# A decode block on one core: first loads issued ahead of the critical section, the store waited for by ScalarE behind it

## The chip, the cores and the metric

The kernel runs on one core of one Trainium2 chip. The metric is the device time of one execution in microseconds. The kernel before takes 400.61 us in the median of three runs (400.36 to 400.88). One execution was profiled; all rows below come from it.

## What is computed

One token (batch 1, sequence 1, D = 1024) goes through a residual sum of two branches, both fed by the layernorm of `x`: attention over a key/value cache of 65,536 positions with 32 query heads on 4 key/value heads of 128, and an MLP mixer with its own layernorm.

```python
xn = _layernorm(x, axis=-1)
return x + _A_ref(xn, A_k_cache, A_v_cache, A_wq, A_wo) + _B_ref(xn, B_w1, B_w2, B_w3, B_w4)

# _A_ref: q = xn @ wq; scores = q k^T * Dh**-0.5; p = softmax(scores); o = p v; o @ wo
# _B_ref: h = gelu(layernorm(xn) @ w1), its four quarters shifted along the sequence, @ w2 = hs
#         (with one position each shift leaves only the zeros of the padding);
#         x1 = xn + hs;  x1 + gelu(layernorm(x1) @ w3) @ w4
```

Everything is bf16 in memory. The caches hold 134 MB and the weights some 35 MB, and each byte is used once.

## The kernel before, in words

The five engines are programmed by hand inside one critical section (`tile_critical`, line 226): semaphores are waited for and counted by the helper class `Flow`. Its method `one` records an instruction of VectorE (V), ScalarE (S) or GpSimd (G); `dma` (line 99, the issue is line 102) a transfer issued by an engine's queue, which adds 16 to a semaphore named by `lane` when it has landed; `_wait` (the wait is line 71) puts a wait ahead of an instruction when it reads or overwrites something that another engine or a transfer has still to finish. TensorE's program is written separately (`tensor_program`, from line 279) as loops that take tokens.

SBUF holds three slots of 32,768 bf16 per partition (64 KB a partition, 8 MB each): C, A, B. All large data passes through them, and SP issues all large loads, in this order: wq into A; w3 into C; the larger part of w4, and w2, into B; then, when wq has been used, w1 and the first rows of w4 into A; when w3 has been used, the first K tile into C; then V, K, K, V and so on by tiles of 32,768 keys (`load_tile`); last, wo in seven pieces into C. A load waits on SP until the products that read the slot's old content have ended (`load`).

The input `x` is loaded twice, both on ScalarE's queue: as one row of 1024 on one partition (`xr`, 2 KB in one piece), and in columns (`x_bf`, 128 partitions of 8 elements, 16 bytes each). From the row, ScalarE, GpSimd and VectorE make the mean and the variance of two nested layernorms (lines 408 to 418), TensorE spreads the four numbers to all partitions (line 281), ScalarE copies them out (line 422). GpSimd then normalises the columns (line 423) into `xn` and `cols`, and gives TensorE a token as soon as these and wq are there. TensorE multiplies by wq (line 286, `row_product` with A), then by w3 (again line 286, with C), and later the other weights (line 307); then come the eight K/V tiles (lines 330 and 345), wo (lines 307, 363, 367), a copy by ScalarE (line 599) and the store (`out`, ScalarE's queue).

Around the section stand parts that the framework makes: a start barrier of all engines behind four memsets (attributed to line 620), the section's entry (a NOP on SP, on which the other engines' branch into the section waits, lines 226 and 631), its exit (a drain of each engine but GpSimd, waits on SP, a NOP on GpSimd and one on SP, line 226), and the final barriers (line 631). The last thing that GpSimd does in the section is to wait until the store has landed.

## Time and profile before

| what | value |
|---|---|
| median of 3 runs | 400.61 us |
| the profiled execution | 400.84 us |
| its span, first to last instruction | 398.7 us |
| TensorE, VectorE, ScalarE, GpSimd busy | 251.5, 205.7, 48.9, 19.1 us |
| moved from HBM | 169.87 MB, 426 GB/s over the span |
| wq load: issued, landed | 0.95, 22.90 us |
| row of x: issued, landed | 0.90, 2.58 us |
| columns of x: issued, landed | 1.49, 25.00 us |
| store: issued, landed | 396.03, 397.70 us |
| granted TensorE clock, mean | 0.867 |

In the timeline, a row holds start, duration, engine, line, operation, what it writes and reads, count, and in brackets the idle time of the engine before it and what ended it; `SPq` and `ACTq` are the sequencers that issue transfers. In the windows, a row holds the window, its length, busy time of PE, PEld, DVE, ACT and POOL with their instruction counts, the granted clock, the DMA share and GB/s. In the DMA view, q1 is SP's queue and q10 ScalarE's, with packets, megabytes and the time that the packets took as a share of the 16 engines. A wait's row holds who waited for whom, the total in us, how often, and the longest.

### The profile page before, as it was taken

What the parts mean: (1) busy time and instruction counts of PE and PEld (TensorE: products, weight loads), DVE (VectorE), ACT (ScalarE), POOL (GpSimd) and SP (SyncE); (2) the same over time, 40 slices, a digit from 0 to 9 for tenths busy, and PEclk for the clock granted to TensorE, in tenths of its full rate; (3) what the DMA queues carried; (4) which work ended last, traced back from release to release, by engine and by line L of the source; (5) the groups of instructions that cost most, each with busy time, mean ns of one, the idle gap of its engine ahead of it and who ended that gap; (6) DMA issues with size and microseconds to landing.
All of it is one profiled execution on the core that took longest, in us unless ns stands there. A gap on an engine that the chain in (4) does not pass through costs nothing. (4 is left out here: it accounts for less than half of the span.)

```text
span 398.7 us, 4662 instructions
## 1 busy us (share of the span) xinstructions
PE 251.5 (63%) x1458; PEld 115.5 (29%) x1458; DVE 205.7 (52%) x135; ACT 48.9 (12%) x87; POOL 19.1 (5%) x58
## 2 busy tenths in 40 slices
PE   0039781997860985198429833981598169779685
PEld 0014330443340432044104411440244024423341
DVE  0000603039625954695079428940993398598510
ACT  5200117200020011002000200020003000300301
POOL 4030000000000003000000030000002000000000
PEclk9999995899985898599858985997698759989999
DMA  8999999999999999999999999999999999999995
GB/s 349 460 401 447 394 436 459 421 421 480 460 427 421 421 421 421 421 487 460 421 421 421 421 421 421 487 460 421 421 421 421 421 427 454 434 421 421 437 423 244
DMA packets 4618, 169.88 MB, mean 426 GB/s; under 512 B 645, under 2 KB 649, under 8 KB 906
## 3 DMA queue, kind: packets, MB, share of 16 engines
q1 hardware_dynamic: 4464, 169.87, 98.7%
q10 hardware_dynamic: 154, 0.01, 0.0%
HBM read 169.87 MB, written 0.00 MB: 426 GB/s over the span
## 5 line engine op out<-in xcount | busy, mean ns | idle before, releaser
L546 DVE STREAM_TRANSPOSE home<-home 128x4096 f32<-128x4096 f32 (+1 forms) x41 | 140.0, 3475 | 68.2 <-DMA home<-in_A_k_cache_dram 68.2
L330 PE MATMUL banks<-home,qst 128*128 x512 | 126.6, 409 | 76.8 <-PEq L277 76.4
L330 PEld LDWEIGHTS banks<-home,qst 128*128 128x128 bf16 x512 | 52.1, 102 | 150.8 <-issue 99.3
L554 ACT ACTIVATE scratch<-m 1x128 f32<-1x128 f32 x8 | 2.5, 308 | 244.7 <-DVE m L553 244.7
L345 PE MATMUL banks<-home,scratch 128*32 128x512 bf16 x512 | 31.4, 398 | 1.4 <-PEq L277 1.2
L307 PE MATMUL banks<-home,cols 128*33 x128 | 29.8, 392 | 2.5 <-PEq L277 2.5
L564 DVE STREAM_TRANSPOSE scratch<-scratch 128x1024 bf16<-128x1024 bf16 x16 | 19.9, 1245 | 17.1 <-ACT scratch L560 17.1
L319 PE MATMUL banks<-ident_f 128*128 128x128 f32 x118 | 26.0, 348 | 0.0
L286 PE MATMUL banks<-home,xn 128*33 x64 | 16.0, 418 | 12.4 <-PEq L277 12.4
L319 PEld LDWEIGHTS banks<-ident_f 128*128 128x128 f32 x118 | 19.3, 213 | 5.2 <-issue 1.2
L345 PEld LDWEIGHTS banks<-home,scratch 128*32 128x32 bf16 x512 | 15.0, 101 | 15.4 <-issue 6.0
L307 PEld LDWEIGHTS banks<-home,cols 128*33 x128 | 12.8, 100 | 18.9 <-issue 6.2
L560 ACT ACTIVATE scratch<-banks,sm 128x1024 bf16<-128x1024 f32 x16 | 17.8, 1113 | 0.5
L463 DVE CAST scratch<-banks 1x2048 bf16<-1x2048 f32 x1 | 2.3, 2279 | 29.2 <-PE banks L286 29.2
L474 POOL COPY qst<-qsel 32x32 bf16<-32x32 bf16 x16 | 3.3, 205 | 268.7 <-DVE sm L512 239.6
L550 DVE TENSOR_REDUCE sm<-banks 128x1 f32<-128x1536 f32 x8 | 13.9, 1738 | 1.2 <-PE banks L330 1.2
L286 PE MATMUL banks<-home,cols 128*33 x56 | 12.2, 379 | 3.0 <-PEq L277 3.0
L286 PEld LDWEIGHTS banks<-home,xn 128*33 128x33 bf16 x64 | 6.8, 106 | 21.3 <-issue 14.9
L551 DVE TENSOR_REDUCE sm<-banks 128x1 f32<-128x512 f32 x8 | 5.5, 692 | 12.6 <-PE banks L330 12.6
L526 DVE SCALAR_TENSOR_TENSOR scratch<-banks,sm,scratch 128x128 f32<-128x128 f32 x16 | 5.6, 350 | 12.0 <-POOL scratch L522 6.5
L487 DVE STREAM_TRANSPOSE scratch<-scratch 32x3584 bf16<-32x3584 bf16 x1 | 3.9, 3899 | 13.5 <-ACT scratch L480 13.5
L281 PE MATMUL banks<-sm,ident_f 1*128 1x4 f32 x2 | 0.6, 345 | 13.7 <-PEq L277 13.7
(91 smaller groups left out, 83.7 us busy)
## 6 DMA issues: line engine op xcount, KB each, us to landing
home<-in_A_k_cache_dram SPq DMA_DIRECT2D x2, 4096.0 KB, 40.8
home<-in_A_v_cache_dram SPq DMA_DIRECT2D x2, 4096.0 KB, 22.3
home<-in_B_w_dram SPq DMA_DIRECT2D x1, 7168.0 KB, 38.4
home<-in_B_w_dram SPq DMA_DIRECT2D x1, 6144.0 KB, 52.5
home<-in_B_w_dram SPq DMA_DIRECT2D x2, 2048.0 KB, 39.1
home<-in_A_wo_dram SPq DMA_DIRECT2D x2, 2048.0 KB, 33.5
home<-in_A_wo_dram SPq DMA_DIRECT2D x3, 1024.0 KB, 39.7
home<-in_B_w_dram SPq DMA_DIRECT2D x1, 1024.0 KB, 23.3
```

What stands on the lines that cost most here:

```text
L286: ins = te.matmul(banks[0:33, bank:][:, bass.ds(ch, 1), :], lhsT=lhsT[:, c:c + 1].to_broadcast([P, 33]), rhs=slot(s)[:, bass.ds(ch * 512 + ...
L307: ins = te.matmul(dst(h), lhsT=lv[:, u:][:, bass.ds(c, 1)].to_broadcast([P, 33]), rhs=wv[:, u * NOUT + h * NH:][:, bass.ds(c * NOUT, NH)], ...
L319: te.matmul(bank[:, 0:P], lhsT=ident_f[:], rhs=ident_f[:], start=True, stop=True, skip_group_check=True)
L330: ins = te.matmul(sc[:, bass.ds(hf, 1), :], lhsT=qst[:, bp, 24 - 8 * cg:24 - 8 * cg + P], rhs=kv[:, bass.ds(r * (2 * 4 * HF) + hf * 4 + cg ...
L345: ins = te.matmul(oacc[32 * u:32 * (u + 1), :], lhsT=work[:, 32 * y:32 * (y + 1)], rhs=vt[:, hf, :, t, :], start=(y < 4), stop=(y >= 60), ...
L487: v(["row0"], ["turned"], lambda e: e.transpose(out=rows32[:, 0:F], in_=rows32[:, 0:F]), tok="VT", peek=["rep4"])
L526: v(["oacc", "wm", "og"], ["og"], lambda e: e.scalar_tensor_tensor(out=og[:, 0:P], in0=oacc[:, P * cg:P * (cg + 1)], scalar=wm[:, 1, cg:cg ...
L546: v([], [("kt", ks, hf)], lambda e: e.transpose(out=part, in_=part), tok="VT", n=n, peek=[("slot", ks, piece_of("K", t, hf)), "qst"], guar ...
L550: v(SC[0:3] + ["sm0"], ["mx2"], lambda e: e.reduce_max(out=mx2[:, 0:1], in_=sc[:, 0:3, :].rearrange("p h n -> p (h n)"), axis=AX.X))
L551: v(SC[3:4], ["mx2b"], lambda e: e.reduce_max(out=mx2[:, 1:2], in_=sc[:, 3, :], axis=AX.X), tok="VT", guard=["pm"])
L560: s(SC + [("nball", r)], [("work", h), "row0", "row1", "turned", ("lall", r, h)], lambda e: e.activation(out=workv[:, 2 * h:2 * h + 2], in ...
L564: v([("work", h)], [("work", h)], lambda e: e.transpose(out=workv[:, 2 * h:2 * h + 2], in_=workv[:, 2 * h:2 * h + 2]))
```

## The change

Three loads leave the section. They are issued in the block ahead of it: the columns of `x` on ScalarE's queue, wq on SP's, the row of `x` on ScalarE's behind the columns. Before, ScalarE issued the row first. They carry the same semaphores as before; they take no waits. A NOP on SP stands behind them as the fence on which the framework lets later work depend. `Flow` and the helpers `slot` and `lane` are made before the section, not in it.

At the other end, GpSimd no longer waits for the store inside the section. ScalarE does so in the block behind it. For the framework's sake GpSimd adds 16 to the store's semaphore ahead of the section and takes them off as its first step in it, so that the count at the store is what it was.

```diff
-    section = ExitStack()
-    section.enter_context(tc.tile_critical(no_gpsimd_drain=True))
     fl = Flow(nc, ctx)
...
+    def early(eng, lane, writes, out, in_):
+        ins = fl.engines[eng].dma_start(out=out, in_=in_).then_inc(fl.sem(lane), 16).ins
+        fl.counts[lane] += 16
+        fl._note((lane, fl.counts[lane]), [], writes)
+        tc.no_tile_sem_insts.add(ins.name)
+        tc.add_to_no_dep_group("early", ins)
+
+    early("S", "x", ["x_bf"], x_bf[:], A_x[0, 0, :].rearrange("(p c) -> p c", c=DC))
+    early("Q", lane(A), [("slot", A, 0)], slot(A), wq_v)
+    early("S", "xr", ["xr"], xr[:], A_x[0])
+    gate = nc.sync.nop()
+    tc.keep_in_program_order(gate)
+    tc.declare_fence(gate.ins, group="early")
+
+    out_done = fl.sem("out")
+    nc.gpsimd.sem_inc(out_done, 16)
+    section = ExitStack()
+    critical = section.enter_context(tc.tile_critical(no_gpsimd_drain=True))
+    nc.gpsimd.sem_inc(out_done, -16)
...
     fl.sem("slot0"), fl.sem("slot1"), fl.sem("slot2")
-    load(A, [(0, wq_v)])
-    fl.dma("S", "xr", [], ["xr"], xr[:], A_x[0])
-    fl.dma("S", "x", [], ["x_bf"], x_bf[:], A_x[0, 0, :].rearrange("(p c) -> p c", c=DC))
     load(C, [(0, w3_v)])
...
-    fl._wait("G", ["out"], [])
     section.close()
+    done = nc.scalar.wait_ge(out_done, 16)
+    tc.add_manual_dep(done.ins, critical.name, mybir.DependencyInfo(mybir.DependencyClass.NoSync, mybir.DependencyReason.DATA),
+                      reason="behind the section")
```

## The prediction

> **What bounds the kernel now.** I read the page's second and third parts first (busy tenths and DMA queues), then the windows, to see whether any stage is short of transfers.

> ```profile
> DMA  8999999999999999999999999999999999999995
> q1 hardware_dynamic: 4464, 169.87, 98.7%
> 1.90:394.90 393.00, 250.90 (x1442) 115.18 (x1442) 205.66 (x135) 48.52 (x86) 18.11 (x54) 0.87 1.00 432
> 394.90:398.70 3.80, 0.63 (x16) 0.31 (x16) 0.00 (x0) 0.37 (x1) 0.00 (x0) 1.00 0.00 1
> ```

> Between 1.9 and 394.9 us the 16 DMA engines are busy without a break (share 1.00, 432 GB/s); TensorE and VectorE are busy 251 and 206 us of 399. The time is therefore 1.9 us of head, 393.0 us of transfer, 3.8 us of tail. Only two things move it: a shorter head or tail, or a hole in the transfers. What the loads at the head gate was read from the timeline of the first microseconds, SP's timeline and the waits.

> ```profile
> 0.90 0.54 ACTq L102 DMA_DIRECT2D xr<-in_A_x_dram  x1
> 0.95 0.37 SPq L102 DMA_DIRECT2D home<-in_A_wq_dram  x1
> 1.49 0.38 ACTq L102 DMA_DIRECT2D x_bf<-in_A_x_dram  x1
> 4.35 1.05 ACT L408 ACTIVATE scratch<-xr 1x1024 f32<-1x1024 bf16 x1
> 14.30 0.16 ACT L422 COPY sm<-banks 128x4 f32<-128x4 f32 x1 [0.92 <-PE banks L281]
> 25.10 0.35 POOL L423 TENSOR_SCALAR lnb<-x_bf,sm 128x8 f32<-128x8 bf16 x1 [12.88 <-DMA x_bf<-in_A_x_dram]
> 26.69 16.04 PE L286 MATMUL banks<-home,xn 128*33 x64 [12.43 <-PEq L277]
> 58.03 0.33 SPq L102 DMA_DIRECT2D home<-in_A_k_cache_dram  x1
> ```

> The row `xr` feeds the layernorm chain (L408 to L422, 10.1 us); the columns `x_bf` are waited for at L423. The first TensorE product starts at 26.69, 1.6 us after L423; its end frees the slot of wq, and the end of the w3 product frees the slot that the first K tile is loaded into, at 58.03.

> **Why the columns land so late.** Four windows of the DMA view, each about one 65,536-byte wq packet long (rows of q1, then of q10, ScalarE's queue):

> ```profile
> q1 hardware_dynamic: 16, 1.05, 100.8%
> q10 hardware_dynamic: 16, 0.00, 0.4%
> ...
> q1 hardware_dynamic: 32, 0.92, 265.6%
> q10 hardware_dynamic: 32, 0.00, 2.2%
> ```

> The first pair is the window 7.3 to 9.7 (9.7 to 12.1 reads the same), the second 21.9 to 22.7. In 2.42 us each of the 16 engines moves one wq packet and one 16-byte packet of the columns: the queues take turns, packet by packet. The columns are 128 packets, 8 an engine, and one that counts: 9 turns. Issued 1.49, they landed at 25.0. The row, one packet on one engine plus its count, was issued 0.05 us ahead of wq, went first (at 1.83, wq's packets from 1.94 on) and landed at 2.58.

> [...] The windows show one descriptor a turn.

> **The change, part by part.**

> *Head.* SP and ScalarE leave the start barrier (L620) at 0.650 and 0.654 by the trace. Before, both pass the section's entry (SP's NOP at 0.72, a branch at 0.75 to 0.79) and issue at 0.95 and 0.90. After, the issues come straight behind the barrier; between two instructions lie about 50 ns, so near 0.72 on both. Gain of the wq stream: 0.23 us, bounds 0 and 0.25. The w3 load, behind wq on SP, passes a NOP and the entry: some 0.1 us later than 1.37, covered by wq's 21 us. GpSimd gets two semaphore additions and the others enter after SP's issue: memset 1.09 to about 1.7. Its cover is the wait at L423 (12.9 us); uncovered it would be 0.6 us of the chain.

> *Tail.* ScalarE issues the store at 396.03, it lands at 397.70. Then GpSimd's branch (397.73), its NOP (397.90), SP's NOP (397.94) and drains reach the final barrier at 398.11.

> ```profile
> SPq L226 <- POOLq L226: 0.7, 1, 0.7
> ```

> After, the section closes while the store flies (ScalarE's drain already ended at 397.17), and ScalarE's wait ends at about 397.73; one instruction later, at 397.8, it signs the barrier. Behind the wait stand only the final drains. GpSimd leaves the barrier at 397.87 instead of 398.11: gain 0.24 us. If ScalarE has to drain again (316 ns at 396.85), the loss is 0.08; bounds -0.08 and 0.3.

> *Order of the three loads.* The columns now start ScalarE's queue, and the row stands behind them. Within one queue the row cannot pass: it needs the columns' 9 turns plus 2 of its own, unless the columns are through before wq's packets arrive. Eight tiny packets need about 8 x 11 ns (two columns packets at 21.96 and 21.97 lie 11 ns apart): a lead of some 90 ns. Before, the row had 44 ns, and needed one packet. Now SP leaves the barrier 4 ns ahead of ScalarE; at both later barriers (398.233 against 398.237, 398.669 against 398.673) the same. The time from issue to first packet was 0.93 us on ScalarE (row) and 0.99 on SP. No row shows the columns against an idle queue, so the price is bounded: nothing if they win, all turns if wq is in first. By the 4 ns I take wq first.

> Then, on the row's engine: columns 1 to 8 after wq packets 1 to 8 (the last at about 22.2), their count beside wq's, one w3 packet (2.12 us), the row at 24.3, one w3 packet, the row's count at 26.4, seen 0.35 later; less 0.23 of head, **26.5**. From there 10.1 us of chain and 1.7 to TensorE: 38.4 in place of 26.7, 11.7 us late. The w1 load into wq's slot (42.83 to 54.5) still arrives before the queue is empty at 59. The K load does not: 58.03 + 11.7 = 69.7. The queue before it ends at 65.5 to 65.9 (landings of the last w4 piece 66.06 to 66.50, less 0.37 of count, less 0.23). A load into an idle queue starts as if 1.66 to 2.25 us after issue (wq: issued 0.95, first packets end at 5.03 to 5.62, one packet is 2.42): 71.4 to 72.0. **Hole: 6.0 us.** The next load, V, would come at 75.84 + 11.7 = 87.5 against K's end near 91.5: no second hole, and K/V loads later are 8 us early as before. Nothing downstream gives the hole back, since the transfers set the end.

> Sum: -0.23 - 0.24 + 6.0 = +5.5 us. The profiled execution took 400.84 (span 398.73, 2.1 us around it), so 406.3; the median is 0.23 lower: **406.1**. Columns one packet ahead of wq: the row one turn earlier, 404.0. A second wq packet already committed, as before the change, when the first column packet came after two: one turn later, 408.2.

> **The rivals.**

> *The columns get through first* (the other side). If ScalarE's packets lead on the row's engine by 90 ns, the row takes two turns and lands near 7.5, the chain ends at about 18, the columns are there, and the product waits for wq alone (landing 22.9): it starts 3 us earlier. That buys nothing, as the queue is full until 66. It decides from the point where the row lands before about 20.6: 26.69 + 5.8 us of spare for K (65.7 less 58.03 + 1.66, less the head's 0.23), less 11.85. For it: ScalarE's 0.93 us from issue to first packet, shorter than SP's 0.99, and that the row did get ahead from a start 44 ns earlier. Against: now ScalarE starts 4 ns later, and has to get nine packets through on the row's engine where the row needed two. Time: 400.61 - 0.47 = **400.1**. [...]

> *A lead of two to five packets.* The row lands between 17 and 22.2; hole 0 to 1.6 us, time 400.1 to 401.7.

> *The section's entry waits for the early loads.* SP could issue w3 only at 22.7, into an empty queue: about 2 us. GpSimd would start 21.6 us late, TensorE at 38: hole near 5.7 as above. Time about 408. For it: the NOP that stands as a fence for the loads. Against: before, the entry is one 13 ns NOP that waits for nothing, and the loads carry semaphores of their own.

> **How the numbers follow.** Row late, by whatever number of turns: 0.58 (404.0: 0.12; 406.1: 0.34; 408.2: 0.12). Columns first: 0.29. Small lead: 0.08, half of it within 0.8 us of before. Entry waits: 0.05. Cases of both signs hold most of the chance: the forecast's own range is 403.5 to 408.5, the range given is 399.9 to 407.3, which leaves out the latest turn and the waiting entry. About 0.2% (0.8 us) can be told from no change: 0.47 us of gain stays within it unless measurement adds 0.3, so faster 0.06, same 0.29, slower 0.65.

> **What would show it.** Right: L408 starts after 24 us, TensorE's first product near 38, the K load near 70, DMA digits below 9 around slice 7, then a chain as before; q10 with 16 packets per 2.4 us from 5 us on. Wrong: L408 near 5 us, product at 23, no hole. Head: wq issued near 0.72, w3 right behind. Tail: from landing to the last instruction about 0.75 us in place of 1.0, ScalarE's wait among the last. If the w3 issue moves past 20 us, the entry waits.

## The result, and the profile after

The changed kernel takes 406.69 us in the median of 6 runs (406.28 to 408.82), against 400.59 us (400.36 to 400.88) for the kernel before in 6 runs beside it: a ratio of 1.0162 [1.0146, 1.0179]. It is 1.6% slower. The profiled execution took 408.33 us (span 406.4, that of before 398.7). Its runs lie on two levels, four between 406.28 and 406.86 and two at 408.33 and 408.82; where the 2 us between them come from is taken up below.

The page's DMA digits, then the windows of the profile after (window, length, busy time of PE, PEld, DVE, ACT and POOL, granted clock, DMA share, GB/s):

```profile
DMA  9989994999999999999999999999999998999996
```

```profile
1.70:66.50 64.80, 25.31 (x99) 11.00 (x100) 7.01 (x4) 9.95 (x14) 9.00 (x29) 0.97 0.99 421
66.50:72.70 6.20, 5.49 (x26) 2.25 (x23) 0.00 (x0) 0.66 (x2) 0.29 (x2) 1.00 0.00 0
72.70:402.80 330.10, 226.04 (x1319) 104.55 (x1320) 198.79 (x131) 37.95 (x71) 9.68 (x24) 0.82 1.00 432
402.80:406.40 3.60, 0.62 (x16) 0.29 (x16) 0.00 (x0) 0.37 (x1) 0.00 (x0) 0.88 0.00 1
```

The one low digit inside the span, a 4 in the seventh slice (61 to 71 us), is a stretch of 6.2 us in which no transfer is in flight. Ahead of it and behind it the engines are as busy as before, and after 72.7 us they run without a break to the end. The head (1.70 in place of 1.9) and the tail (3.60 in place of 3.8) are each shorter by 0.2 us. So the loss is one hole, which nothing later gives back. The landings show it: the first K tile lands at 93.45 instead of 85.87 (+7.58), the last piece of wo at 403.11 instead of 395.26 (+7.86). The gap in which nothing is in flight is shorter than the loss, because the 16 engines do not stop and restart all at once: they end their last w4 packets between 65.52 and 66.50 us, and 14 of the 16 first K packets take 2.79 to 3.30 us in place of 2.42. In the mean an engine stops at 65.8, and its first K packet ends at 76.0, as if it had started at 73.6: 7.8 us are lost.

The timeline of the profile after, with the instructions that answer to those shown of before (start, duration, engine, line, what it writes and reads; in brackets the idle time ahead of it and what ended it):

```profile
0.73 0.37 SPq L237 DMA_DIRECT2D home<-in_A_wq_dram  x1
0.73 0.41 ACTq L237 DMA_DIRECT2D x_bf<-in_A_x_dram  x1
1.18 0.53 ACTq L237 DMA_DIRECT2D xr<-in_A_x_dram  x1
1.45 54.62 SPq L102 DMA_DIRECT2D home<-in_B_w_dram  x5
...
26.88 1.06 ACT L425 ACTIVATE scratch<-xr 1x1024 f32<-1x1024 bf16 x1 [21.96 <-DMA xr<-in_A_x_dram]
...
37.17 0.35 POOL L440 TENSOR_SCALAR lnb<-x_bf,sm 128x8 f32<-128x8 bf16 x1 [2.42 <-ACT sm L439]
38.77 16.41 PE L303 MATMUL banks<-home,xn 128*33 x64 [1.98 <-PEq L294]
58.15 13.54 PE L303 MATMUL banks<-home,cols 128*33 x56 [2.97 <-PEq L294]
71.76 0.33 SPq L102 DMA_DIRECT2D home<-in_A_k_cache_dram  x1
```

(The lines of the section have moved down by 17: L408 is L425 now, L423 is L440, L286 is L303.) The columns and wq are issued in the same hundredth of a microsecond. ScalarE then waits 21.96 us for the row, which lands at 26.86 where it landed at 2.58. L440, which waited for the columns before, now waits for the chain that starts at the row. Everything up to the K load has moved by the same 12 to 14 us: the first product from 26.69 to 38.77, the K load from 58.03 to 71.76. No piece ahead of the K load is in flight after 66.50, so the queue ran dry before SP was allowed to refill it.

The DMA view of the profile after in the window 4.7 to 7.1 us, one wq packet long (queue, packets, megabytes, share of the 16 engines):

```profile
q1 hardware_dynamic: 16, 1.05, 100.8%
q10 hardware_dynamic: 16, 0.00, 0.4%
```

On each of the 16 engines one 65,536-byte packet of wq goes, and then one of the columns' 16-byte packets. The first column packet goes at 4.83, behind one wq packet; the columns land at 22.94, the row's packet goes at 24.33, and its count at 26.52.

### The profile page after: what moved, and what is told of

Its sections match the earlier page's. It is cut to its first block, busy times and chain, and to the rows that moved or that the text cites. A ratio compares the mean times of both kernels' runs of the same rounds, so it can differ in the third digit from the quotient of the medians.

```text
span 406.4 us, 4665 instructions
## 1 busy us (share of the span) xinstructions
PE 257.5 (63%) x1458; PEld 118.1 (29%) x1458; DVE 205.8 (51%) x135; ACT 48.9 (12%) x87; POOL 19.2 (5%) x58
## 3 DMA queue, kind: packets, MB, share of 16 engines
q1 hardware_dynamic: 4464, 169.87, 97.1%
HBM read 169.87 MB, written 0.00 MB: 418 GB/s over the span
## 5 line engine op out<-in xcount | busy, mean ns | idle before, releaser
L362 PE MATMUL banks<-home,scratch 128*32 128x512 bf16 x512 | 33.0, 413 | 0.7 <-PEq L294 0.6
L324 PE MATMUL banks<-home,cols 128*33 x128 | 31.8, 415 | 1.6 <-PEq L294 1.6
L581 DVE STREAM_TRANSPOSE scratch<-scratch 128x1024 bf16<-128x1024 bf16 x16 | 19.9, 1246 | 17.1 <-ACT scratch L577 17.1
L336 PE MATMUL banks<-ident_f 128*128 128x128 f32 x118 | 27.3, 380 | 0.0
L336 PEld LDWEIGHTS banks<-ident_f 128*128 128x128 f32 x118 | 21.6, 246 | 3.8 <-issue 0.5
L362 PEld LDWEIGHTS banks<-home,scratch 128*32 128x32 bf16 x512 | 14.4, 104 | 17.1 <-issue 7.9
L303 PE MATMUL banks<-home,xn 128*33 x64 | 16.4, 425 | 2.0 <-PEq L294 2.0
L303 PE MATMUL banks<-home,cols 128*33 x56 | 13.5, 406 | 3.0 <-PEq L294 3.0
L543 DVE SCALAR_TENSOR_TENSOR scratch<-banks,sm,scratch 128x128 f32<-128x128 f32 x16 | 5.6, 350 | 12.3 <-POOL scratch L539 6.5
```

Source lines behind the costliest of these rows:

```text
L303: ins = te.matmul(banks[0:33, bank:][:, bass.ds(ch, 1), :], lhsT=lhsT[:, c:c + 1].to_broadcast([P, 33]), rhs=slot(s)[:, bass.ds(ch * 512 + ...
L324: ins = te.matmul(dst(h), lhsT=lv[:, u:][:, bass.ds(c, 1)].to_broadcast([P, 33]), rhs=wv[:, u * NOUT + h * NH:][:, bass.ds(c * NOUT, NH)], ...
L336: te.matmul(bank[:, 0:P], lhsT=ident_f[:], rhs=ident_f[:], start=True, stop=True, skip_group_check=True)
L362: ins = te.matmul(oacc[32 * u:32 * (u + 1), :], lhsT=work[:, 32 * y:32 * (y + 1)], rhs=vt[:, hf, :, t, :], start=(y < 4), stop=(y >= 60), ...
L543: v(["oacc", "wm", "og"], ["og"], lambda e: e.scalar_tensor_tensor(out=og[:, 0:P], in0=oacc[:, P * cg:P * (cg + 1)], scalar=wm[:, 1, cg:cg ...
L581: v([("work", h)], [("work", h)], lambda e: e.transpose(out=workv[:, 2 * h:2 * h + 2], in_=workv[:, 2 * h:2 * h + 2]))
```

## The experiments

Where a median is given for the kernel before, it is that of runs beside it on the same chip.

### The row first again, all else as changed

```diff
-    early("S", "x", ["x_bf"], x_bf[:], A_x[0, 0, :].rearrange("(p c) -> p c", c=DC))
-    early("Q", lane(A), [("slot", A, 0)], slot(A), wq_v)
     early("S", "xr", ["xr"], xr[:], A_x[0])
+    early("Q", lane(A), [("slot", A, 0)], slot(A), wq_v)
+    early("S", "x", ["x_bf"], x_bf[:], A_x[0, 0, :].rearrange("(p c) -> p c", c=DC))
```

> The changed kernel with one edit: ScalarE issues the row ahead of the columns, all three loads still ahead of the section, the store still waited for by ScalarE. Theory of the order (the row pays the columns' turns because it stands behind them): the row lands before 3 us, the columns near 24.8, TensorE's first product starts near 26.5, no hole, and the two small gains at head and tail are left: 400.2 us (400.0 to 400.4), 0.1% below the kernel before. Rival (the loads' place ahead of the section, or the fence, is what costs): 406 to 407 as in the changed kernel.

Measured: 400.50 us (400.24 to 400.86, 11 runs) against 400.87 (400.37 to 401.61, 21 runs), ratio 0.9992 [0.9983, 1.0002]. The timeline of this run:

```profile
0.73 0.52 ACTq L237 DMA_DIRECT2D xr<-in_A_x_dram  x1
...
24.82 0.35 POOL L440 TENSOR_SCALAR lnb<-x_bf,sm 128x8 f32<-128x8 bf16 x1 [12.02 <-DMA x_bf<-in_A_x_dram]
26.42 16.23 PE L303 MATMUL banks<-home,xn 128*33 x64 [11.56 <-PEq L294]
60.84 0.33 SPq L102 DMA_DIRECT2D home<-in_A_k_cache_dram  x1
```

The row lands at 2.02, L440 waits for the columns again, and the queue never runs dry. The median is 0.37 us below that of the kernel before, near the 0.4 expected, though 400.50 itself lies above the range given, since the kernel before took 400.87 on this chip; and the interval of the ratio holds no change. The order of two lines of code carries the whole 6 us; issuing ahead of the section costs nothing that can be told.

### The order alone, inside the section

The kernel before, with its two loads of `x` changed over:

```diff
     load(A, [(0, wq_v)])
-    fl.dma("S", "xr", [], ["xr"], xr[:], A_x[0])
     fl.dma("S", "x", [], ["x_bf"], x_bf[:], A_x[0, 0, :].rearrange("(p c) -> p c", c=DC))
+    fl.dma("S", "xr", [], ["xr"], xr[:], A_x[0])
```

> The kernel before with one edit: inside the section ScalarE issues the columns ahead of the row. Here ScalarE issues some 44 ns ahead of SP. Theory of the order: 44 ns is less than the 90 ns that eight packets need, so the columns still take turns with wq, the row lands between 22 and 27 us, a hole of 1.6 to 8 us opens ahead of the first K tile, 402 to 408 us. Rival (the place ahead of the section costs): 400.6 us. Rival (any lead lets the columns through): the row lands near 7 us, 400.6 us and TensorE's first product near 23.5.

Measured: 407.67 us (406.24 to 408.95, 4 runs), ratio 1.0157 [1.0128, 1.0187]. The timeline:

```profile
0.90 0.43 ACTq L102 DMA_DIRECT2D x_bf<-in_A_x_dram  x1
...
26.62 1.05 ACT L408 ACTIVATE scratch<-xr 1x1024 f32<-1x1024 bf16 x1 [22.29 <-DMA xr<-in_A_x_dram]
...
72.02 0.33 SPq L102 DMA_DIRECT2D home<-in_A_k_cache_dram  x1
```

Here the columns were issued at 0.90 and wq at 0.95, a lead of 0.05 us. It bought not one packet: the first column packet still went behind one wq packet (4.99), on every engine. The order by itself gives the whole loss. Here too the runs lie on two levels, 406.24 and 406.39, 408.94 and 408.95.

### The end alone

The kernel before, with only the second half of the change: ScalarE waits for the store behind the section.

```diff
+    out_done = fl.sem("out")
+    nc.gpsimd.sem_inc(out_done, 16)
...
+    nc.gpsimd.sem_inc(out_done, -16)
...
-    fl._wait("G", ["out"], [])
...
+    done = nc.scalar.wait_ge(out_done, 16)
```

> The kernel before with the tail's half of the change alone: GpSimd's two semaphore steps, no wait of GpSimd for the store, ScalarE waits for it behind the section. From the landing of the store to the last instruction 0.86 us in place of 1.03, as in the changed kernel: 400.4 us (400.2 to 400.6). Rival (the two steps of GpSimd and the wait cost more than they save): 400.6 or above.

Measured: 400.69 us (400.33 to 401.37, 11 runs), ratio 0.9998 [0.9989, 1.0007]. From the store's landing to the last instruction the trace has 0.859 us in place of 1.030. These 0.17 us are there, but too small to tell from no change in the time. This run shows something else as well, in its timeline:

```profile
46.55 13.78 PE L290 MATMUL banks<-home,cols 128*33 x56 [2.96 <-PEq L281]
60.41 0.33 SPq L102 DMA_DIRECT2D home<-in_A_k_cache_dram  x1
```

The w3 product took 13.78 us at a mean granted clock of 0.89 (12.25 in the profile before, at 1.00), and the K load was issued 2.4 us later than before (0.85 of it was there when the product began). The span is 398.55 us all the same: the queue was not yet empty.

### The columns in two halves, the row between them

After, with 64 partitions of the columns, the row, and then the other 64; GpSimd's normalisation waits for both.

```diff
-    early("S", "x", ["x_bf"], x_bf[:], A_x[0, 0, :].rearrange("(p c) -> p c", c=DC))
+    early("S", "x", ["x_bf"], x_bf[0:64], A_x[0, 0, 0:512].rearrange("(p c) -> p c", c=DC))
     early("Q", lane(A), [("slot", A, 0)], slot(A), wq_v)
     early("S", "xr", ["xr"], xr[:], A_x[0])
+    early("S", "x2", ["x_bf2"], x_bf[64:128], A_x[0, 0, 512:1024].rearrange("(p c) -> p c", c=DC))
```

> The changed kernel with the columns loaded in two halves of 64 partitions, ScalarE's queue holding first half, row, second half. Theory of turns (each small packet costs one wq packet of 2.42 us): on the row's engine 4 packets and a count stand ahead of the row in place of 8 and a count, so the row lands 7 us earlier than in the changed kernel, near 19.9; the chain ends near 30, the second half of the columns lands near 28.7, TensorE's first product starts near 31.7, some 1 us before the point from which the K load comes too late: no hole, 400.1 to 400.8 us. Rival (ScalarE's queue is simply served when wq is through): the row lands at 24 or later, 404 us or more.

Measured: 404.78 us (404.96, 404.72, 402.31, 404.84), ratio 1.0076 [1.0048, 1.0104]: slower than expected. The timeline, then the DMA view of the windows 4.7 to 7.1 and 7.1 to 9.5 us:

```profile
0.73 0.57 ACTq L237 DMA_DIRECT2D x_bf<-in_A_x_dram  x1
...
22.35 1.05 ACT L426 ACTIVATE scratch<-xr 1x1024 f32<-1x1024 bf16 x1 [17.42 <-DMA xr<-in_A_x_dram]
...
67.72 0.33 SPq L102 DMA_DIRECT2D home<-in_A_k_cache_dram  x1
```

```profile
q1 hardware_dynamic: 16, 1.05, 100.8%
...
q1 hardware_dynamic: 16, 1.05, 100.8%
q10 hardware_dynamic: 16, 0.00, 0.4%
```

In the first window ScalarE's queue has no packet at all. The issue of 64 partitions took 0.57 us (0.41 for 128), and the first column packet went behind two wq packets (7.18) instead of one. From there on the count of turns holds: column packets at 7.2, 9.6, 12.0 and 14.4, their count at 16.9, the row at 19.39, the row's count at 21.99. There are four turns less of columns, one more at the front, and one for the columns' count, which in the profile after had gone beside wq's own count (22.08 to 22.43). That makes two turns less: the row landed 4.5 us earlier than in the profile after, at 22.33. By the prediction's point of decision (20.6) that is 1.7 us too late; to these the w3 product, 1.4 us longer than at full clock, adds its part, and the stretch without a packet in flight was 2.8 us (65.88 to 68.69). The expectation failed in the first turn, not in the rule. The one run at 402.31 has no profile, and why it is 2.5 us shorter stays open.

### A lead for the columns

SP takes four steps, additions to a semaphore that nobody waits for, ahead of wq's issue; a second kernel takes ten. wq's issue is held to the program's order behind these steps; that part of the edit is left out here.

```diff
...
+    for _ in range(4):
+        tc.keep_in_program_order(nc.sync.sem_inc(fl.sem("idle"), 1))
     early("Q", lane(A), [("slot", A, 0)], slot(A), wq_v)
```

> The changed kernel with four semaphore steps on SP ahead of wq (76 ns each in the changed kernel's trace), so that ScalarE issues the columns some 0.3 us ahead of wq. With 44 ns of lead they still took every turn. Theory of the race (eight tiny packets need a lead of some 90 ns at the DMA engines): the columns land before 3 us, the row after two turns near 7, TensorE's first product starts when wq has landed, near 23.8, no hole, 400.5 us. Rival (the columns' packets reach the engines later after their issue than wq's, by more than 0.3 us): the row still lands near 27, 406.5 to 409 us.

> The same with ten steps, a lead of about 0.76 us. Theory of the race: the columns are through, the row after two turns near 7.5, no hole, the head 0.76 us longer than in the changed kernel: 400.9 us. Rival (ScalarE's queue is served behind wq whatever its lead): the row lands near 27, 407 us or more.

Measured with four: 400.71 us (400.40 to 400.98, 10 runs), ratio 0.9996 [0.9986, 1.0006]; with ten: 400.97 (400.67 to 401.36, 10 runs), ratio 1.0005 [0.9996, 1.0015]. The timeline with four steps, then its DMA view of the window 1.6 to 2.4 us:

```profile
0.73 0.40 ACTq L237 DMA_DIRECT2D x_bf<-in_A_x_dram  x1
0.98 0.37 SPq L237 DMA_DIRECT2D home<-in_A_wq_dram  x1
8.28 1.05 ACT L430 ACTIVATE scratch<-xr 1x1024 f32<-1x1024 bf16 x1 [3.10 <-DMA xr<-in_A_x_dram]
23.39 15.27 PE L308 MATMUL banks<-home,xn 128*33 x64 [5.19 <-PEq L299]
```

```profile
q1 hardware_dynamic: 13, 0.85, 317.3%
q10 hardware_dynamic: 144, 0.00, 9.1%
```

The lead came out at 0.25 us (0.3 expected). With it all 144 packets of the columns (128 of data, 16 that count) go between 1.75 and 2.04 us, the last of them among the first packets of wq. The columns land at 2.39, the row costs two turns (8.25), and the first product waits only for wq. It starts 3.3 us earlier than in the kernel before, and the time is the same: the transfers were already without a break. With ten steps (lead 0.61, 0.76 expected) the row too got ahead of wq (2.47; it was expected near 7.5), and wq started 0.36 us later.

### The changed kernel once more

No edit: a second profile of the kernel after, to see whether its two levels come from the clock.

> The changed kernel once more, unedited, for a second profile. Theory on its two levels of time (four runs at 406.3 to 406.9, two at 408.3 and 408.8): with the hole, the K load waits for the w3 product, so a stretch of half the granted clock in that product moves the time. A profile without such a stretch before the K load has the w3 product at 12.3 us in place of 13.5, the K load near 70 in place of 71.8 and takes 406.3; one with it repeats 408.3. Rival (the two levels come from the transfers): the times do not follow the clock's record.

Measured, in one execution: 407.19 us, span 405.4. Its w3 product and its K load in the timeline:

```profile
57.57 12.25 PE L303 MATMUL banks<-home,cols 128*33 x56 [2.96 <-PEq L294]
69.89 0.33 SPq L102 DMA_DIRECT2D home<-in_A_k_cache_dram  x1
```

Now the window at the start of the w3 product: first in the execution of 408.33 us (of the engines, this row shows TensorE alone), then in this one:

```profile
57.40:60.80 3.40, 2.65 (x7) 0.50 1.01 424
```

```profile
57.60:60.80 3.20, 3.20 (x15) 1.49 (x16) 3.20 (x1) 0.00 (x0) 0.00 (x0) 1.00 1.01 430
```

In the first, TensorE's granted clock was 0.50 for 3.4 us, and only 7 multiplications started in the 2.65 us of it that the product saw; in the second it was 1.00, and 15 started in 3.2 us. The product began at 58.15 in the first, 0.75 us into the half-clock stretch; from 60.8 us on the clock was 1.00 in both. The product took 12.25 instead of 13.54 us, and the K load was issued at 69.89 instead of 71.76. Of these 1.87 us the product gives 1.29; the row landed 0.38 earlier (26.48), and the wq product was 0.21 shorter. The stretch without a packet was 4.8 us (66.03 to 70.86) instead of 6.2. The K tile landed 5.96 us later than in the kernel before (7.58 in the other execution). So far the expectation held, with the clock as the larger part of the difference and not the whole. The time did not come down to 406.3, though: the last piece of wo was 6.83 us late, 0.87 more, without which it would be 406.3. Four of the 65,536-byte packets around 91 us took more than 2.6 us, up to 2.98, in place of 2.42. What made them slow wasn't tried and stays open.

### The row on SP's queue, ahead of wq

After, with the row's load moved from ScalarE's queue to SP's:

```diff
+    early("Q", "xr", ["xr"], xr[:], A_x[0])
     early("Q", lane(A), [("slot", A, 0)], slot(A), wq_v)
-    early("S", "xr", ["xr"], xr[:], A_x[0])
```

> The changed kernel with the row issued by SP ahead of wq; ScalarE's queue holds the columns alone, still issued at 0.73 us. Theory of the order within a queue: the row stands behind nothing and lands before 3 us; wq is issued some 0.57 us later (the row's issue takes 0.53), which gives the columns a lead of more than 0.25 us, so they are through as well; TensorE's first product starts near 23.9, no hole: 400.8 us, the head 0.35 us longer than in the kernel before and the tail 0.17 shorter. Rival (columns ahead of the row cost by themselves, in whichever queue): 404 us or more.

Measured: 400.78 us (400.38 to 401.04, 10 runs) against 400.81, ratio 0.9997 [0.9987, 1.0007]. From the timeline, wq's issue:

```profile
1.13 0.36 SPq L237 DMA_DIRECT2D home<-in_A_wq_dram  x1
```

The row's issue on SP (0.34 us) gives the columns, issued at 0.73, a lead of 0.40 us (0.57 was expected, from the 0.53 that the issue takes on ScalarE's queue); the row landed at 2.10, the columns at 2.38, and there was no hole. The cost is wq, issued 0.40 us later than in the kernel after.

None of these kernels is measurably faster than the kernel before. The nearest is the row first with both ends of the change kept, ratio 0.9992 [0.9983, 1.0002]: its profiled span is 398.25 us in place of 398.73, but the interval still holds no change.

## Why the prediction was right

Forecast 406.1 us, measured 406.69, by the mechanism forecast. There is luck in the closeness: the range given ends at 407.3, two of the six runs lie above it, and the median lies in it because four fell on the lower level. By the prediction's own steps:

**The transfers set the end.** Confirmed from both sides. With the columns first the hole appears in the time almost microsecond for microsecond; and an earlier first product (23.39 in place of 26.69, with four steps of lead: 400.71 us) or a later K load (60.84 in place of 58.03, with the row first: 400.50) changes nothing as long as the queue is not empty.

**The race and the turns.** Right. wq went first, the columns cost one wq packet (2.42 us) for each of their packets on an engine, and the row was seen at 26.86, in the second profile at 26.48 (forecast 26.5). The 4 ns of the barrier, by which the prediction took wq first, did not decide it: both issues start at 0.732, and a lead of 0.05 us for the columns loses as well. The outcome was right by a wider margin than the working had. "Eight tiny packets need a lead of some 90 ns" was the weakest working: 0.05 us bought not a single packet, and 0.25 us bought all 144, which ran over 0.29 us. Where between these two the lead decides wasn't tried. While both queues have packets, the window from 4.7 to 7.1 us shows the engines taking them in turn: 16 of wq and 16 of the columns in 2.4 us, so that each 16-byte packet waits for its own turn.

**The chain behind the row.** Forecast 38.4 for the first product; 38.77 in the profiled execution, 38.40 in the second one. The K load was forecast at 69.7: 69.89 at full clock, 71.76 with the stretch at half clock. The prediction took the w3 product at the 12.3 us of one profile; it lasts 13.5 us and more when a stretch at half clock falls into it, and as soon as the K load waits for it with the queue empty, the difference is in the time. A later turn of the columns is not what made the two profiled runs on the upper level long (408.33, and 408.95 with the order alone): their rows landed at 26.86 and 26.60, and both have the half-clock stretch, worth 1.29 and 1.47 us. The levels lie 2 to 2.7 us apart, and no run near 406.3 has a profile, so what makes up the rest of the distance stays open.

**The hole.** Forecast 6.0 us. The K tile landed 5.96 us late at full clock, 7.58 with the half-clock stretch. The restart "as if 1.66 to 2.25 us after issue" holds: the first K packets, less 2.42 us, start as if 1.50 to 2.00 us after the issue in the first profile and 1.64 to 2.25 in the second. The queue's end was forecast 0.23 us earlier than before: the last w4 piece landed 0.19 earlier in the second profile (66.31 against 66.50) and 0.30 later in the first (66.81). No second hole came; V was issued at 90.81, K landed at 93.45. One sum is off: the point up to which the row may land takes the head's 0.23 us off twice, as 65.7 already has it, so 20.6 should read 20.9; the forecast does not use it.

**Head and tail.** The head is as forecast: wq issued at 0.73 in place of 0.95 (0.22 us of 0.23), GpSimd's memset at 1.68 (1.7). The tail was mis-sized: from landing to the last instruction 0.86 us in place of 1.03, a gain of 0.17 of the 0.24 forecast, since ScalarE signs the barrier 0.17 us after its wait has ended, not 0.07. In the waits, SP's row for ScalarE reads:

```profile
SPq L253 <- ACTq L253: 1.5, 1, 1.5
```

This wait of 1.5 us stood in the exit before as well (L226). What has gone is the wait of 0.7 us for GpSimd behind it: SP's exit NOP ran at 397.94 before, 0.24 us after the landing, and runs at 405.10 now, 0.47 us ahead of it.

**The rivals.** "The columns get through first" is a real regime, which the leads of 0.25 us and more show; the change did not reach it. Its time of 400.1 has no run of its own: with four steps 400.71 was measured, but there wq is issued at 0.98, so that the head's gain is spent on the lead. "A lead of two to five packets" was not met in any run; with the columns in two halves the row landed just behind it, at 22.33. "The section's entry waits" falls: the first load issued inside the section, w3, starts at 1.45, right behind wq.

## What to carry to other kernels

In this kernel a load of many small pieces beside a stream of large ones paid one large packet (2.42 us) per piece on each engine, and the row, queued behind it on the same queue, waited for all of them (it landed at 26.86 in place of 2.58). Put what a long chain waits for first, and the load with many small pieces behind it, or give it a measured lead (here 0.25 us was enough). Before a load is moved, compare how much later its consumer may start until a queue downstream runs dry (here, by the prediction's estimate, some 18 us after the row's old landing at 2.58). Within it a delay was free (5.7 us with four steps of lead); beyond it (19.8 us with the columns in two halves, 24.3 in the changed kernel) each microsecond counts, as does each stall of an engine that was hidden until then (here the 1.29 us that the stretch at half clock added to the w3 product).
